# Transposing q and k on VectorE instead of TensorE: sliding-window attention with a gMLP block, one core

## The chip, the cores and the metric

The kernel runs on one core of one Trainium2 chip. The metric is the device time of one execution in microseconds (us). Most executions of one kernel agree within a few tenths of a per cent to one per cent. An execution more than 1.5% above the fastest of its kernel counts as slow; ratios below use the others ("fast runs") alone. The medians that are quoted are over all runs of a kernel, slow ones included; they hold one slow run in e6, e8, e11 and e17, two in e15, and none elsewhere.

PE is TensorE (matmuls), PEld its weight loads, DVE is VectorE, ACT is ScalarE, POOL is GpSimd, SP is SyncE, which only issues transfers. HBM is the memory outside of the core, SBUF the memory inside it, PSUM the accumulators behind PE.

## The reference, cut to what matters

Eight batches, eight heads, 576 tokens, 64 features per head. A token attends to itself and to the 63 tokens before it; a gMLP block with a spatial mixing matrix over the tokens follows.

```python
q, k, v: (8, 8, 576, 64) fp32, normal * 0.1
scores = q @ k.T / 8, kept where 0 <= i - j < 64
x      = softmax(scores) @ v, heads side by side: (8, 576, 512)
h      = relu(x @ w_in)                  # w_in (512, 1024)
u, v   = h[..., :512], h[..., 512:]
v_n    = (v - mean) / sqrt(var + 1e-6)
v_s    = w_spatial @ v_n + b_spatial     # w_spatial (576, 576)
out    = (u * v_s) @ w_out               # w_out (512, 512)
```

A score is a sum of 64 products of order 0.01, some 0.08 in size, divided by 8; so the scores are near zero and the softmax is nearly uniform over the window. **The comparison with the reference cannot see a wrong order of q's and k's tokens.**

## The kernel before

A batch goes through five attention steps (T transposes, S scores, E exponential and mask, P weighted values and denominators, N normalization to x), four of which take two heads each; the fifth takes the last 64 queries of all heads. Then come V and U (the halves of h), LN, G (spatial mixing, times u) and O (output). From the third batch on, the PE stream interleaves the attention of batch i, V, U and G of batch i−1 and O of batch i−2.

q, k and v come in as fp32, 256 bytes at a time, and are cast to fp16 by POOL (by ACT and DVE for the first batch). PE transposes q and k, DVE copies the result out of PSUM, and the scores contract 64 features in one matmul:

```python
def emit_T(b, s):                        # cut: the remainder step s == 4
    tp = psp.tile([128, 1024], f16, tag="tp", bufs=1, ...)
    for c in range(4):
        nc.tensor.transpose(tp[:, 512+128*c:640+128*c], Kh[:, c, 2*s:2*s+2, :], id16[:, :])
    for c in range(4):
        nc.tensor.transpose(tp[:, 128*c:128*c+128],     Qh[:, c, 2*s:2*s+2, :], id16[:, :])
    qk = apool.tile([128, 1024], f16, tag="qk", bufs=6, ...)
    nc.vector.tensor_copy(qk[:, :], tp[:, :])
...
# emit_S: 16 matmuls a step, on 64-row tiles of the array
for h in (0, 1):
    d = slice(64*h, 64*h+64)
    nc.tensor.matmul(sc[r:r+64, h, c0:c1], qk[d, 512+64*kap:576+64*kap], qk[d, c0:c1], ...)
...
# order of a steady iteration
st[2] += [LN] + [U0, U1] + [G0];  st[3] += [U2, G1, U4, G2];  st[4] += [U3, G3, G4]
...
# emit_O
nc.scalar.copy(ob[0:jn, :], po[0:jn, :])                      # ob: 3 buffers
(nc.scalar if b < 2 else nc.sync).dma_start(out[...], ob[0:jn, :])
```

The softmax here doesn't subtract the row's maximum and nothing guards it: scores larger than these inputs give would overflow.

## Time and profile before

The median is 251.62 us (251.4 to 252.29, three runs).

| Reading | Value | View of the profile |
|---|---|---|
| busy PE / DVE / ACT / POOL | 227 / 155 / 152 / 122 of 249.3 us | page, part 1 |
| one steady iteration (first V matmul to the next batch's) | 25.9 us, PE busy 25.6 | windows |
| first V matmul of batch 0 / of batch 1 | 30.1 / 71.3 us | timeline of PE |
| longest PE wait | 4.4 us near 64 us | waits |
| eight transposes of a step on PE | 0.45 us | timeline of PE |
| sixteen score matmuls of a step | 0.35 us | timeline of PE |

From the page of the kernel before: busy times with instruction counts; then the span in 40 slices with a digit for tenths busy, for PE, DVE, the granted clock of PE and the DMA; then two DMA queues with packets, MB and share of the DMA engines' time.

```profile
PE 227.3 (91%) x2588; PEld 116.8 (47%) x2588; DVE 155.3 (62%) x317; ACT 152.2 (61%) x266; POOL 122.1 (49%) x183
...
PE   7784996996399999999999999999999999999893
...
DVE  6453277562459782887479556966597659755630
...
PEclk9999799799569999999999999999999999999998
DMA  8999999999999996992389948995499040014005
...
q1 hardware_dynamic: 114720, 34.88, 70.1%
q0 software_dynamic: 1840, 2.24, 5.2%
```

A slice is 6.2 us. PE is full from the 12th slice (69 us) on, so a steady iteration is worth what its PE work is worth. Ahead of that PE has gaps, the granted clock is lower after the longest of them (digits 5 and 6, 62 to 75 us), and the DMA is busy throughout.

The windows view of the kernel before, one steady iteration (stretch, length, busy time and count of PE, PEld, DVE, ACT, POOL, granted clock, DMA share, GB/s). A DMA share may read over 1.

```profile
150.60:176.50 25.90, 25.57 (x317) 13.23 (x315) 19.11 (x36) 17.78 (x32) 14.96 (x20) 1.00 0.85 183
```

The timeline of PE before (start, duration, instruction, count): the transposes of one step and what follows, and the scores of one step and what follows. The difference of two starts is what a group costs the stream.

```profile
97.89 0.40 PE L210 MATMUL tp_2_1850<-id_130,hk_1219 128*128 128x128 f16 x4
98.12 0.39 PE L213 MATMUL tp_2_1850<-id_130,hq_1218 128*128 128x128 f16 x4
98.34 0.38 PE L330 MATMUL pv_0_1862<-win_179,x_0_1397 128*128 128x512 f16 x1
...
146.62 0.42 PE L242 MATMUL sc_0_2882<-qk_0_2745 64*64 64x128 f16 x16
146.97 0.30 PE L281 MATMUL oz_4_2900<-e2r_2802,onesK 128*64 128x256 f16 x2
```

The transposes cost 98.34 − 97.89 = 0.45 us of PE, the scores 146.97 − 146.62 = 0.35 us. This is what the change wants to trade.

### The profile page before, as it was taken

The numbers are of one execution on the slowest core, as the hardware profiler recorded it, in microseconds if no ns is written. First come the engines' busy times: TensorE is split into PE (matmuls) and PEld (weight loads), VectorE is DVE, ScalarE is ACT, GpSimd is POOL, SyncE is SP. The second block draws the span as 40 slices with busy tenths as digits, with TensorE's granted clock in tenths as the row PEclk, the third lists the DMA queues.
The fourth block names the chain that finished last, engine by engine and source line by source line (L and its number), as shares of the span: only waits on it lengthen the run. The fifth ranks groups of instructions, "written<-read, shape, count | busy, mean of one in ns | idle before, by whom it ended". The sixth has DMA issues, their size and how long they took to land.

```text
span 249.3 us, 6391 instructions
## 1 busy us (share of the span) xinstructions
PE 227.3 (91%) x2588; PEld 116.8 (47%) x2588; DVE 155.3 (62%) x317; ACT 152.2 (61%) x266; POOL 122.1 (49%) x183
## 2 busy tenths in 40 slices
PE   7784996996399999999999999999999999999893
PEld 3442453553254464436544554455445544553351
DVE  6453277562459782887479556966597659755630
ACT  3373484446447666766785577756776677767423
POOL 3469638875499695369016592469135900000000
PEclk9999799799569999999999999999999999999998
DMA  8999999999999996992389948995499040014005
GB/s 159 218 184 208 216 204 229 191 201 276 249 199 210 198 178 175 246 206 52 128 192 211 192 128 221 189 198 135 137 216 156 27 165 5 3 42 149 0 3 189
DMA packets 120014, 40.41 MB, mean 162 GB/s; under 512 B 113776, under 2 KB 114864, under 8 KB 119984
## 3 DMA queue, kind: packets, MB, share of 16 engines
q1 hardware_dynamic: 114720, 34.88, 70.1%
q0 software_dynamic: 1840, 2.24, 5.2%
q10 hardware_dynamic: 3424, 2.88, 4.1%
q8 instruction: 20, 0.33, 0.6%
q14 instruction: 10, 0.08, 0.1%
HBM read 32.79 MB, written 9.44 MB: 169 GB/s over the span
## 4 chain that ended last, share of the span: by engine, by line
PE 60%; DVE 13%; ACT 9%; DMA 8%; SPq 3%; POOL 2%; issue 2%; ACTq 1%; POOLq 0%
SPq L68 3%; DMA nv_80<-in_v_dram 2%; DMA out_dram<-ob_0_1033 2%; DMA out_dram<-ob_1_3433 2%; DMA nq_78<-in_q_dram 2%; ACTq L407 1%; PE ps_0_804 L382 1%; PE warm_583 L114 1%; PE pv_0_1308 L330 1%; PE ps_0_4590 L382 1%; PE ps_0_4237 L382 1%; DVE mv_172 L336 1%; PE ps_0_3720 L382 1%; PE ps_1_895 L382 0%; PE ps_3_4653 L382 0%
## 5 line engine op out<-in xcount | busy, mean ns | idle before, releaser
L88 POOL CAST hq_2281<-nq_2285 128x512 f16<-128x512 f32 (+1 forms) x5 | 3.2, 635 | 12.8 <-DMA nq_2285<-in_q_dram 12.8
L114 PEld LDWEIGHTS <-scratch 128*128 128x128 f16 x51 | 5.0, 112 | 7.3 <-issue 3.8
L88 POOL CAST hq_3389<-nq_3393 128x512 f16<-128x512 f32 (+1 forms) x5 | 3.9, 797 | 8.8 <-DMA nq_3393<-in_q_dram 8.8
L281 PEld LDWEIGHTS <-onesK 128*64 128x64 f16 x80 | 4.6, 107 | 7.5 <-issue 5.2
L88 POOL CAST hq_2835<-nq_2839 128x512 f16<-128x512 f32 (+1 forms) x5 | 3.6, 720 | 8.3 <-DMA nq_2839<-in_q_dram 8.3
L176 ACT CAST hk_109<-nk_79 128x512 f16<-128x512 f32 x4 | 2.5, 618 | 7.5 <-DMA nk_79<-in_k_dram 7.5
L114 PE MATMUL warm_113<-scratch 128*128 128x512 f16 x16 | 5.5, 524 | 1.3 <-DVE scratch L109 1.3
L81 POOL CAST hv_110<-nv_80 128x512 f16<-128x512 f32 x4 | 2.5, 632 | 8.3 <-DMA nv_80<-in_v_dram 7.3
L88 POOL CAST hv_1729<-nv_1733 128x512 f16<-128x512 f32 (+1 forms) x5 | 3.5, 708 | 4.4 <-DMA nv_1733<-in_v_dram 4.4
L88 POOL CAST hq_1727<-nq_1731 128x512 f16<-128x512 f32 (+1 forms) x5 | 2.9, 609 | 4.6 <-DMA nq_1731<-in_q_dram 4.6
L88 POOL CAST hv_2283<-nv_2287 128x512 f16<-128x512 f32 (+1 forms) x5 | 3.2, 637 | 3.8 <-DMA nv_2287<-in_v_dram 3.8
L81 POOL CAST hv_433<-nv_437 128x512 f16<-128x512 f32 x4 | 2.5, 613 | 5.2 <-DMA nv_437<-in_v_dram 5.1
L88 POOL CAST hv_1184<-nv_764 128x512 f16<-128x512 f32 (+1 forms) x5 | 3.1, 611 | 3.9 <-DMA nv_764<-in_v_dram 3.9
L362 PEld LDWEIGHTS <-win_181 128*128 128x128 f16 x32 | 3.1, 98 | 3.8
L362 PEld LDWEIGHTS <-win_182 128*128 128x128 f16 x32 | 3.1, 98 | 3.8
L88 POOL CAST hv_1220<-nv_1224 128x512 f16<-128x512 f32 (+1 forms) x5 | 3.9, 780 | 2.0 <-DMA nv_1224<-in_v_dram 2.0
L88 POOL CAST hq_1182<-nq_762 128x512 f16<-128x512 f32 (+1 forms) x5 | 3.3, 654 | 3.2 <-DMA nq_762<-in_q_dram 2.7
L81 DVE CAST hq_108<-nq_78 128x512 f16<-128x512 f32 x4 | 1.7, 432 | 4.8 <-DMA nq_78<-in_q_dram 4.8
L281 PE MATMUL oz_3_1153<-e_1_3_1108,onesK 128*64 128x512 f16 x2 | 0.6, 611 | 4.4 <-DVE x_2_1133 L308 4.4
L88 POOL CAST hv_3391<-nv_3395 128x512 f16<-128x512 f32 (+1 forms) x5 | 3.0, 611 | 2.8 <-DMA nv_3395<-in_v_dram 2.8
L88 POOL CAST hv_2837<-nv_2841 128x512 f16<-128x512 f32 (+1 forms) x5 | 3.3, 666 | 2.0 <-DMA nv_2841<-in_v_dram 1.8
L264 ACT ACTIVATE e_1_0_831<-sc_0_813 128x1024 f16<-128x1024 f32 x1 | 1.0, 1023 | 5.2 <-PE sc_0_813 L242 5.2
(1871 smaller groups left out, 940.3 us busy)
## 6 DMA issues: line engine op xcount, KB each, us to landing
nk_79<-in_k_dram SPq DMA_DIRECT2D x9, 128.0 KB, 3.9
nq_78<-in_q_dram SPq DMA_DIRECT2D x9, 128.0 KB, 4.1
nk_436<-in_k_dram SPq DMA_DIRECT2D x9, 128.0 KB, 4.8
nq_435<-in_q_dram SPq DMA_DIRECT2D x9, 128.0 KB, 4.8
nv_437<-in_v_dram SPq DMA_DIRECT2D x9, 128.0 KB, 4.1
nk_763<-in_k_dram SPq DMA_DIRECT2D x4, 256.0 KB, 5.5
nq_762<-in_q_dram SPq DMA_DIRECT2D x4, 256.0 KB, 5.7
nv_764<-in_v_dram SPq DMA_DIRECT2D x4, 256.0 KB, 6.0
```

Source lines behind the costliest of these rows:

```text
L68: eng.dma_start(NAT[b][x][:, 0:4, h, :], SRC[x][b, h, 0:512, :].rearrange("(c p) d -> p c d", p=128))
L81: eng.tensor_copy(F16[b][x][:, 0:4, hs, :], NAT[b][x][:, 0:4, hs, :])
L88: eng.tensor_copy(F16[b][x][0:sn, c, :, :], NAT[b][x][0:sn, c, :, :])
L114: nc.tensor.matmul(t[:, :], scratch[:, 0:128], scratch[:, :], start=True, stop=True)
L176: nc.scalar.copy(o, i)
L264: nc.scalar.activation(e2[:, :, :], sc[:, :, :], AF.Exp, bias=0.0, scale=0.125)
L281: nc.tensor.matmul(oz[64 * h:64 * h + 64, 1, 0:n], onesK[:, :], e2[:, h, 0:n], start=True, stop=True)
L330: nc.tensor.matmul(pv[0:jn, :], xcol(b, r, j), w_in_sb[r][:, 512:1024], start=(r == 0), stop=(r == 3))
L336: nc.vector.bn_aggr(mv_t[b % NSB][0:jn, j, :], st6[0:jn, 0:6])
L362: nc.tensor.matmul(pu[:, :], w_in_sb[r][:, 128 * m:128 * m + 128], X[b, r][:, :], start=(r == 0), stop=(r == 3))
L382: nc.tensor.matmul(ps[:, :], VN[b, kk][0:kn, 128 * m:128 * m + 128], wspT[kk][0:kn, 0:512], start=(kk == 0), stop=(kk == 4))
L407: (nc.scalar if b < 2 else nc.sync).dma_start(out[b, 128 * j:128 * j + jn, :], ob[0:jn, :])
```

## The change

Intent: take the transposes off PE and the casts of q and k off POOL, and read HBM in long rows.

- q and k are loaded with 18 consecutive tokens per partition (4.6 KB of fp32 in a row) and cast to fp16 by the DMA itself.
- DVE transposes them in 32x32 blocks. A partition holds tokens 18·i to 18·i+17, so one block gives tokens c, 18+c, 36+c, ... of 32 features. To put the tokens in order, the output is written with a step of 18 elements, 36 bytes.
- DVE leaves the 64 features of a head in two sets of 32 rows, so each score product becomes a pair of 32-row matmuls that accumulate.
- In a steady iteration G comes behind nearly all of U.

```diff
-    def emit_T(b, s): ... nc.tensor.transpose(...) ... nc.vector.tensor_copy(qk, tp)
+    def load_qk(b, x, hp):
+        s = SRC[x][b, 4*hp:4*hp+4, :, :].rearrange("g (i c) d -> (g i) (c d)", c=18)
+        nc.gpsimd.dma_start(NAT[b, x][:, hp, :, :, :].rearrange("p c e d -> p (c e d)"), s)
+
+    def turn(b, x, hp, half):
+        cs = slice(9 * half, 9 * half + 9)
+        o = TR[b, x][:, hp, :, :].rearrange("p e (i c) -> p c e i", c=18)
+        nc.vector.transpose(o[:, cs, :, :], NAT[b, x][:, hp, cs, :, :])
...
+        return [lambda e=e: nc.tensor.matmul(
+            out, TR[b,"k"][rows, hp, e, 64*key:64*key+64], TR[b,"q"][rows, hp, e, q0:q1],
+            start=(e == 0), stop=(e == 1), tile_position=(32*g, r)) for e in (0, 1)]
...
-            st[2] += [LN] + [U0, U1] + [G0];  st[3] += [U2, G1, U4, G2];  st[4] += [U3, G3, G4]
+            st[2] += [LN] + [U0, U1, U2];     st[3] += [G0, U3, G1, U4];  st[4] += [G2, G3, G4]
...
-        ru = mpool.tile([128, 512], f32, tag="ru", bufs=3, ...)
+        ru = mpool.tile([128, 512], f32, tag="ru", bufs=5, ...)
```

(Also cut: a fourth PSUM buffer for U, V, G and O, the two halves of w_in loaded apart, the loads of v and their casts as before but in a new order, and the fill of batch 1's steps, which takes two units of batch 0 ahead of each step instead of one.)

## The prediction

> **What bounds it now.** From 93 to 221 us the kernel is bound by TensorE. In the windows view the four full batch iterations (first output projection to first output projection) last 26.2, 26.1, 25.9 and 25.8 us, with PE busy 25.5 to 25.7 us of each; DVE is busy 18.5, ACT 18. The last batch with attention takes 24.6. At the front, DMA bounds: its share reads over 1.0 up to 93 us, 128 KB loads take 4 to 5 us, and the first V matmul starts at 30.1 us. Between 60 and 64.6 us PE waits 4.4 us for x_2, held behind ACT output copies that wait for 5 us output DMAs; then the granted clock is 0.66 (60 to 75 us).
>
> **PE per iteration (timeline).** Removed: four groups of eight 128-column transposes at 56 ns, 0.45 us each, 1.8 us; the remainder's transposes and the mode change they cause, 0.44. Sum −2.2 us. Added: 32-row pairs double the score matmuls from 16 to 32 per step, still four at once on different tiles. Sixteen now take four groups of 56 ns, so four more groups cost 0.22 us, four times: +0.9. The remainder goes to eight tiles at once, about even. The Trainium skill ("TensorE: Matmul & The Clock Gate", Part 3) says row tiles run concurrently with starts 4 ns apart; today's 64-row score matmuls agree (3 to 4 ns), and the trace has no 32-row ones. Net −1.3.
>
> **G behind U.** G0 takes 1.9 us from its first matmul to the end where its siblings take 1.08: 0.8 lost waiting for the normalized tiles. One more U (0.86) runs in between, but two transposes (instead of one 0.65 us copy) now stand on DVE before normalization: I count −0.4.
>
> **DVE.** Out: copies 3.1 us per iteration. In: eight transposes of 128x576. The trace has none; the skill's "VectorE: DVE Perf Modes" (The three transpose paths) gives 311 ns for 128x128 bf16; with one element per cycle, as a 512-element fp32 copy's 0.69 us suggests, I estimate 0.65 to 0.75 us each, 5.5 in all. DVE rises to about 21 of 24.5 us: not the bound, but g_2 behind two transposes can hold a PSUM slot, +0.3. ACT +0.4 (three exps for the remainder). POOL loses ten casts (about 6 us).
>
> Iteration: 26.0 − 1.3 − 0.4 + 0.3 = 24.6 us. Five iterations (the last 23.5): −7 us. Tail: one U fills the normalization wait, −1.
>
> **Front.** q and k go from 256 B packets to rows of 4.6 KB; the DMA-cast weights moved 2.24 MB (output bytes) in 5.2% of the span, 173 GB/s, so a batch's q and k take some 7 us of DMA instead of 12. First scores about 9.5 us (8.7 now, as four heads must land), then ACT paces some 3 us per step; first V at 24 to 25 instead of 30. Batch 1 waits about 2 us for its eight transposes on DVE. With DMA relieved, the 4.4 us wait and the cold clock after it go. Together −12 us (range −6 to −16).
>
> **Predicted: 232 us**, 8 in 10 within 225 to 241. Faster by over 2%: 0.95; within 2%: 0.04; slower: 0.01.
>
> **What shows it.** Iterations near 24.6 us with PE still over 95%; score steps near 0.48 us of PE; transposes near 0.7 us; first V near 24.5 us; DMA share below 0.8 from 30 us on; no 4 us PE wait near 60 us.
>
> **What would make it wrong.** Transposes with the 36-byte output stride costing over 1.1 us make DVE the bound (25 us per iteration or more); 32-row pairs not overlapping add 0.9 us more per iteration; cast loads slower than 173 GB/s delay the front.

## The result, and the profile after

The changed kernel takes **345.79 us** (344.99 to 347.89, four runs) against 251.84 of the kernel before beside it: ratio 1.3764, 95% interval 1.3703 to 1.3826. It passes the comparison with the reference and is 38% slower. Ratios here and below are the mean time of one kernel's fast runs over that of the other's of the same rounds, so not quite the ratio of the medians that are quoted.

The same lines of the page of the changed kernel, then the chain of work that ended last and two groups of instructions (busy us, mean ns):

```profile
PE 240.2 (70%) x2899; PEld 118.1 (34%) x2899; DVE 279.8 (81%) x329; ACT 152.9 (44%) x283; POOL 87.7 (25%) x138
...
PE   5073885058702767599678967796759695999995
...
DVE  4978359995499699978999799969996999877450
...
PEclk9566999556955699969698989699978969899999
...
q1 hardware_dynamic: 41504, 16.52, 21.0%
q0 software_dynamic: 7024, 11.68, 19.6%
...
DVE 52%; PE 28%; ACT 8%; issue 6%; DMA 3%; POOL 2%; ACTq 0%; POOLq 0%
...
L76 DVE STREAM_TRANSPOSE tq<-nq 128x576 f16<-128x576 f16 x32 | 82.7, 2760 | 0.0
L76 DVE STREAM_TRANSPOSE tk<-nk 128x576 f16<-128x576 f16 x32 | 81.7, 2729 | 0.0
```

DVE went from 155 to 280 us, 52% of the chain is DVE, and the two lines at the end say why: 64 transposes of 2.7 us each, 164 us in all by their durations. The prediction had counted 0.65 to 0.75 us each, some 45 us. The other columns did what was expected: POOL fell from 122 to 88 us and packets from 114,720 to 41,504 on the first queue.

One iteration in the windows view, and the waits of PE (for what, us in total, times, longest):

```profile
189.20:225.80 36.60, 29.16 (x356) 13.86 (x356) 33.98 (x39) 18.18 (x35) 11.05 (x15) 0.86 0.43 98
...
PE sc L202 <- DVE tq L76: 28.2, 3, 12.2
PE oz L265 <- DVE x L293: 22.0, 9, 9.2
PE po L387 <- DVE g L369: 19.2, 9, 3.8
PE ps L366 <- DVE vn L336: 18.9, 9, 3.3
```

An iteration is now 36.6 us with DVE busy 34.0. Only the first wait names a transpose. The others name x, g and vn, small DVE operations that stand in DVE's order behind a pair of transposes (5.1 us): an overloaded engine shows up under the names of whatever queues on it. The granted clock is 0.86 here, with PE pausing; it was 1.00 before and is 1.00 in e2 below, which does the same PE work without these pauses in 24.2 us of busy time. Here PE is busy 29.2 us.

Where the 95.5 us between the two profiled spans (249.3 and 344.8) lie, by the first V matmul of each batch (V0, V1, V7); later rows are explained below. Each row is one profiled execution. Up to the first output, near 55 us, e4 and e18 below are the same program as the kernel before; their V0 is 29.4 and 32.8 us, and V1 of e4 is 69.2. So in this kernel differences of up to some 3 us in V0 or V1 between two profiles are not separated.

| Kernel | V0 | V0 to V1 | V1 to V7 | from V7 to the end | span |
|---|---|---|---|---|---|
| before | 30.1 | 41.2 | 154.8 | 23.2 | 249.3 |
| after | 42.7 | 72.4 | 206.9 | 22.8 | 344.8 |
| e2_contig (no stride, wrong token order) | 27.2 | 47.6 | 147.2 | 22.9 | 244.9 |
| e5_pairs (32-bit words, right order) | 27.1 | 47.7 | 149.0 | 22.9 | 246.7 |
| e17_spout (e5 and a new front) | 27.7 | 31.2 | 149.8 | 22.7 | 231.4 |

### The profile page after: what moved, and what is told of

Same layout as the page of the kernel before. It is cut to its first block, busy times and chain, and to the rows that moved or that the text cites. A ratio compares the mean times of both kernels' runs of the same rounds, so it can differ in the third digit from the quotient of the medians.

```text
span 344.8 us, 6862 instructions
## 1 busy us (share of the span) xinstructions
PE 240.2 (70%) x2899; PEld 118.1 (34%) x2899; DVE 279.8 (81%) x329; ACT 152.9 (44%) x283; POOL 87.7 (25%) x138
## 3 DMA queue, kind: packets, MB, share of 16 engines
q1 hardware_dynamic: 41504, 16.52, 21.0%
q0 software_dynamic: 7024, 11.68, 19.6%
HBM read 32.79 MB, written 9.44 MB: 122 GB/s over the span
## 4 chain that ended last, share of the span: by engine, by line
DVE 52%; PE 28%; ACT 8%; issue 6%; DMA 3%; POOL 2%; ACTq 0%; POOLq 0%
DVE tk L76 18%; DVE tq L76 16%; PE po L387 11%; PE pv L314 5%; DVE x L293 4%; DVE vn L336 4%; PE ps L366 4%; DVE g L369 3%; PE sc L202 3%; DVE st L319 3%; DVE e L251 2%; ACT vs L317 2%; PE oz L265 2%; DMA wnat<-in_moe_w_spatial_dram 2%; PE oz L275 1%
## 5 line engine op out<-in xcount | busy, mean ns | idle before, releaser
L76 DVE STREAM_TRANSPOSE tq<-nq 128x576 f16<-128x576 f16 x32 | 82.7, 2760 | 0.0
L76 DVE STREAM_TRANSPOSE tk<-nk 128x576 f16<-128x576 f16 x32 | 81.7, 2729 | 0.0
L366 PE MATMUL ps<-wspT,vn 128*128 128x512 f16 (+1 forms) x160 | 46.8, 421 | 22.3 <-DVE vn L336 18.9
L387 PE MATMUL po<-wout,g 128*128 128x512 f16 (+1 forms) x160 | 48.4, 446 | 19.2 <-DVE g L369 19.2
L115 POOL COPY vs<-vn 64x1024 f16<-64x1024 f16 (+1 forms) x44 | 40.5, 921 | 60.5 <-PE oz L275 33.4
L242 ACT ACTIVATE e<-sc 128x1024 f16<-128x1024 f32 x32 | 32.7, 1022 | 41.6 <-PE sc L202 40.5
L202 PE MATMUL sc<-tq,tk 32*64 32x128 f16 (+2 forms) x1152 | 29.0, 249 | 28.9 <-DVE tq L76 28.2
L314 PE MATMUL pv<-win,x 128*128 128x512 f16 (+1 forms) x160 | 39.3, 392 | 0.0
L319 DVE BATCH_NORM_STATS2 st<-vs 128x6 f32<-128x512 f16 (+1 forms) x40 | 27.5, 687 | 13.2 <-ACT vs L317 12.8
L346 PE MATMUL pu<-x,win 128*128 128x512 f16 x128 | 33.9, 404 | 0.0
L283 ACT ACTIVATE ln<-oz 128x512 f32<-128x512 f32 (+1 forms) x40 | 22.3, 557 | 25.8 <-PE oz L275 24.6
```

Of the source, the lines that this page charges most:

```text
L76: nc.vector.transpose(o[:, cs, :, :], NAT[b, x][:, hp, cs, :, :])
L115: nc.gpsimd.tensor_copy(o, i)
L202: return [lambda e=e: nc.tensor.matmul(out, TR[b, "k"][rows, hp, e, 64 * key:64 * key + 64], TR[b, "q"][rows, hp, e, q0:q1], start=(e == 0 ...
L242: nc.scalar.activation(e2[:, :, :], sc[0][:, :, :], AF.Exp, bias=0.0, scale=0.125)
L314: nc.tensor.matmul(pv[0:jn, :], xcol(b, r, j), w_in_sb[r][:, 512:1024], start=(r == 0), stop=(r == 3))
L319: nc.vector.bn_stats(st6[0:jn, 0:6], vs[0:jn, :])
```

## The experiments

Theory A for the slowdown: the 36-byte step of the writes makes each transpose slow. Rivals: B, the block transpose is slow by itself in this shape; C, it is slowed by the other engines and the DMA beside it.

### e1_turns: the transposes by themselves

No attention at all: six times each, alone on the core, the transposes of this kernel and variants of them, and plain copies (output wrong, 133.34 us).

```diff
+ for r in (1, 2, 3, 6, 9, 18):                 # tokens per run: step of 2*r bytes
+     nc.vector.transpose(t[:, 0, :].rearrange("p (k i r) -> p k r i", i=32, r=r),
+                         src[:, :, 0, :].rearrange("p (k r) d -> p k r d", r=r))
```

> The VectorE transpose alone, six of each form in a row, nothing else on the chip but the write-out of zeros (the output is wrong on purpose). In the changed kernel a 128x576 fp16 transpose took 2.61 to 2.86 us with a start-to-start pitch of 2.3 to 2.5 us. Theory A (write stride: the output columns of a block lie 18 tokens, 36 bytes, apart, so each write goes to another SBUF line; the Trainium skill, SBUF - State Buffer, names 16-byte lines): the as-is form repeats 2.5 to 2.8 us, contiguous output takes 0.65 to 0.8 us, runs of 2 and 3 tokens (4 and 6 byte steps) also under 0.9 us, 6 tokens (12 bytes) in between, 9 and 18 tokens 2.5 us or more; a plain copy with the 36-byte step is slow as well. Rival B (the transpose itself costs about 4 cycles per element or a fixed 140 ns per 32x32 block, whatever the stride): all fp16 forms of 576 elements take 2.5 us or more, and 128 flat columns take about 0.55 us. Rival C (contention with loads and with GpSimd in the real kernel): even the as-is form takes 0.65 to 0.8 us here.

From the groups of instructions of this run (busy us, mean ns; the first two lines are the kernel's own form with a step of 36 bytes and contiguous, then copies with that step and contiguous, fp32 elements with a step of 72 bytes and contiguous, a step of 36 bytes on the read side only, and 128x128 flat):

```profile
L70 DVE STREAM_TRANSPOSE asis<-src 128x576 f16<-128x576 f16 x6 | 15.8, 2639 | 0.2
L73 DVE STREAM_TRANSPOSE asis<-src 128x576 f16<-128x576 f16 x6 | 4.7, 779 | 0.2
...
L96 DVE COPY copy<-src 128x576 f16<-128x576 f16 x6 | 8.4, 1399 | 0.2
L93 DVE COPY copy<-src 128x576 f16<-128x576 f16 x6 | 1.9, 310 | 0.2
...
L105 DVE STREAM_TRANSPOSE wide<-src 128x576 f32<-128x576 f32 x6 | 7.6, 1258 | 0.2
L101 DVE STREAM_TRANSPOSE wide<-src 128x576 f32<-128x576 f32 x6 | 4.7, 778 | 0.2
...
L89 DVE STREAM_TRANSPOSE readstep<-src 128x576 f16<-128x576 f16 x6 | 7.2, 1199 | 0.2
L82 DVE STREAM_TRANSPOSE flat<-src 128x128 f16<-128x128 f16 x6 | 1.9, 312 | 0.2
```

The steps in between, six transposes each, one by one from the trace: 2 bytes 779 ns, 4 bytes 814, 6 bytes 1132, 12 bytes 2092, 18 bytes 2692, 36 bytes 2640.

Theory A holds and B and C fall. The same transpose takes 779 ns when it writes contiguously and 2639 ns with the kernel's step, alone on the core; the kernel's 2.7 us adds only some 4% for all that runs beside it. The block transpose is not slow by itself: written contiguously it is short, and a plain copy slows with the same step too, from 310 to 1399 ns. But the step adds 1.09 us to the copy and 1.86 us to the transpose, so it is not one cost for both; why stays open. The cost rises with the step and is level from 18 bytes on. One size was forecast wrongly: a step of 6 bytes was to stay under 0.9 us and took 1.13. The width counts too: 4-byte elements at 72 bytes cost 1258 ns, half of what 2-byte elements at 36 bytes cost for the same count, and twice the data.

The Trainium skill ("SBUF — State Buffer", Specifications) says that SBUF has 16-byte lines that need two or more hits each for full bandwidth and that each crossing to a new line pays. The level from 18 bytes on agrees with a line of that size; the rise that starts at 6 bytes, with two or more elements still in a line, does not. The page gives no size of the penalty; here it is 1.9 us per instruction of 576 elements. The skill's "VectorE: DVE Perf Modes" (The three transpose paths) gives 311 ns for 128x128 bf16; the trace has 312 for fp16. The passage cut from the prediction rested the estimate on a copy of 512 fp32 elements in 0.69 us, and no trace shown then has such a copy: the DVE casts of 512 fp32 elements took 0.43 us. The figure that the prediction used was right, but it is that of a contiguous output.

### e2_contig: the changed kernel without the stride

One line of the change differs: tokens are written in the order in which they come. q and k are then permuted in the same way, so the scores pair wrong tokens; the result is wrong and still within tolerance. The times of all engines are those of the real work.

```diff
-        o = TR[b, x][:, hp, :, :].rearrange("p e (i c) -> p c e i", c=18)
+        o = TR[b, x][:, hp, :, :].rearrange("p e (c i) -> p c e i", c=18)
```

> The changed kernel with one line altered: the transposes write contiguous columns (tokens end up in the wrong order, the result is wrong on purpose); every instruction count, size and dependency stays. Theory A: each transpose takes 0.65 to 0.8 us, DVE falls to about 21 us per batch, and the time falls to the predicted 232 us (225 to 241), showing that the rest of the prediction held. Rival B: the transposes stay near 2.75 us and the time near 345 us. Rival D (the transposes are not the only cause: the pairs of 32-row matmuls or the cast loads are slow as well): transposes become short but the time stays above 245 us.

Measured: 247.53 us (246.57 to 248.49, two runs), ratio 0.9857 (0.9782 to 0.9931). From its page (one group), its windows view and its timeline of PE:

```profile
L76 DVE STREAM_TRANSPOSE tk<-nk 128x576 f16<-128x576 f16 x32 | 22.6, 744 | 0.0
...
150.00:174.20 24.20, 24.20 (x355) 12.13 (x354) 19.75 (x38) 17.73 (x35) 10.23 (x15) 1.00 0.69 149
...
151.87 0.64 PE L202 MATMUL sc<-tq,tk 32*64 32x128 f16 x32
152.44 0.41 PE L265 MATMUL oz<-e,onesK 128*64 128x512 f16 x2
```

That one line is worth 98 us, more than the whole loss. The transposes are short as Theory A of the forecast said, but the time is not the forecast 225 to 241 us; it lies over the 245 of Rival D. Without the stride the steady part is what the prediction said: 24.2 us per iteration (24.6 predicted), and 32 score matmuls in 152.44 − 151.87 = 0.57 us against 0.35 for 16, which is the +0.22 us per step of the prediction. (The skill's "TensorE: Matmul & The Clock Gate", Part 3, says that 32-row tiles run concurrently; these 0.57 us agree.) But the kernel gains 1.4% and not 8%: V1 comes at 74.8 us, later than before (71.3). The front, worth −12 us in the prediction, did not come. That is the second question, taken up from e5 on.

### e3_run3: three tokens per partition and row

Loads of runs of three tokens (768 bytes of fp32), so that the step is 6 bytes. This needs four loads where one did. The token order is right by its access patterns.

```diff
-        s = SRC[x][b, 4*hp:4*hp+4, :, :].rearrange("g (i c) d -> (g i) (c d)", c=18)
+        for g in range(4):
+            s = SRC[x][b, 4*hp+g, :, :].rearrange("(k i c) d -> i k (c d)", i=32, c=3)
```

> A correct version: a partition takes runs of 3 tokens (768-byte pieces, six per partition) instead of 18, so a transposed block is written with a 6-byte step. The loads become four per half of the heads, with six times as many pieces for GpSimd to describe. Theory A: transposes under 0.9 us, time between 228 and 245 us, faster than before. Rival B: still about 345 us. If the smaller pieces cost what the 256-byte ones of before did, the front end lies some 5 us behind that of the contiguous variant.

Measured: 267.12 us, ratio 1.0629 (1.0577 to 1.0682), where 228 to 245 us and transposes under 0.9 us were forecast. The transposes take 1.11 to 1.13 us as in e1, and an iteration 25.5 us. The loss is new: POOL issues 128 loads for q and k at 0.57 us each, 72 us in all; V0 comes at 38.4 and V1 at 87.4 us. The group of the k loads (busy us, mean ns):

```profile
L73 POOL DMA_DIRECT2D nk<-in_k_dram x64 | 36.2, 573 | 10.3 <-DMA nk<-in_k_dram 6.0
```

### e4_gorder: the new order of G and U alone

The kernel before with only the order of U and G of the change. Its `ru` tiles keep three buffers, because five don't fit into SBUF there.

```diff
-            st[2] += [LN] + [U0, U1] + [G0];  st[3] += [U2, G1, U4, G2];  st[4] += [U3, G3, G4]
+            st[2] += [LN] + [U0, U1, U2];     st[3] += [G0, U3, G1, U4];  st[4] += [G2, G3, G4]
```

> The kernel before with only the order of G and U changed in batches 1 to 7 (three ru buffers as before, since five do not fit beside its fp32 tiles). My prediction counted 0.4 us per batch, up to 0.8 (the wait of G0 for the normalized tiles), for six full batches and about 1 us in the tail: time 247.5 to 249.5 us, that is 1 to 2% faster than before. If the wait only moves to another place, the time stays within 0.5%.

Measured: 249.24 us, ratio 0.9949 (0.9884 to 1.0015). Its iteration in the windows view is 25.5 us against 25.9, the 0.4 us of the prediction. But that holds for the iterations in the middle only: the first after V1 takes 28.0 us against 27.1, the last 24.5 against 23.8, and V1 to V7 is 154.7 us against 154.8. The new order moved the time and saved none of it there.

### e5_pairs: the change mended, with the tokens in order

DVE moves two fp16 features as one 32-bit word. One transpose then has half as many elements, 4 bytes wide, with a step of 72 bytes. A row holds the even and odd feature of a pair side by side, so a 32-row score matmul takes the even ones, the other the odd ones, each reading with a step of 4 bytes. As the comparison with the reference can't see token order, the layout was worked through with an index model; it puts the tokens of the change and of e5 in order. No run shows it.

```diff
-        o = TR[b, x][:, hp, :, :].rearrange("p e (i c) -> p c e i", c=18)
-        nc.vector.transpose(o[:, cs, :, :], NAT[b, x][:, hp, cs, :, :])
+        o = TR[b, x][:, hp, :, :].rearrange("p t e -> p (t e)").bitcast(f32)
+        n = NAT[b, x][:, hp, :, :].rearrange("p c d -> p (c d)").bitcast(f32)
+        nc.vector.transpose(o.rearrange("p (i c) -> p c i", c=18)[:, cs, :],
+                            n.rearrange("p (c d) -> p c d", d=32)[:, cs, :])
```

> The changed kernel with correct token order and its 4.6 KB load rows, but the transposes move 32-bit words, each a pair of neighbouring fp16 head dimensions: half the columns, 288 per transpose, written with a 72-byte step; the score matmuls then read even and odd dimensions with a 4-byte step. From the isolated forms (576 columns of fp32 with a 72-byte step 1.26 us, flat forms' fixed part about 0.18) I estimate 0.72 us per transpose, as many as before. Theory A (2-byte writes to scattered lines are the cost) expects transposes near 0.75 us and the time of the contiguous variant, 245 to 250 us. If TensorE reads the 4-byte step at half rate, each score step (0.64 us with the next one's wait in the contiguous variant) grows by 0.3 us or more, 1.3 us per batch, and the time is 255 us or more. Rival B (any transpose is slow in the real kernel) fell already with the isolated run.

Measured: 248.82 us, ratio 0.9926 (0.9841 to 1.001). One group and one iteration:

```profile
L77 DVE STREAM_TRANSPOSE tq<-nq 128x288 f32<-128x288 f32 x32 | 19.9, 699 | 0.1
...
151.00:175.60 24.60, 23.99 (x355) 12.46 (x354) 19.11 (x38) 17.71 (x35) 10.20 (x15) 1.00 0.66 146
```

A transpose of the same data takes 0.70 us instead of 2.7, and by the index model the order is right. The iteration is 24.6 us. Its front is that of e2 (V0 27.1, V1 74.8).

### e6_ob6, e7_wsp, e8_pairs_front: two repairs of the front

In e2, PE stands 3.2 us for w_spatial near 35 us, and 4.8 us for x near 66 us, where ACT waits for a buffer of an output copy. e6 is e2 with six output buffers instead of three; e7 is e2 with w_spatial (and the first half of w_in) loaded earlier; e8 is e5 with both.

```diff
-        ob = mpool.tile([128, 512], f32, tag="ob", bufs=3, ...)      # e6, e8: bufs=6
-        if s == 2: load_win(1)
-        if s == 3: load_win(0)
-        if s == 4: load_wsp()
+        if s == 1: load_win(1); load_wsp()                           # e7, e8
+        if s == 2: load_win(0)
```

> The contiguous variant (token order wrong on purpose) with one number changed: six output buffers instead of three. In the contiguous variant ACT stood 3.2 us and then PE 4.8 us from 60.9 us on, since the fourth output copy had to wait for an output DMA among the bursts of prefetch loads, and the cold clock followed. Theory F1 (output buffers cost the front): the 4.8 us wait goes, time 240 to 243.5 us. Rival F2 (the wait is only the symptom of loads that saturate the DMA, another wait takes its place): time within 1.5 us of 247.5.

> The contiguous variant (token order wrong on purpose) with the weight loads issued earlier: the V half of w_in and the spatial weights after step 1, the U half after step 2. In the contiguous variant PE waits from 31.8 to about 36 us for the spatial weights, whose loads GpSimd issues only from 26.0 us on, and batch 1's loads queue behind them. Theory F3: the W transposes follow V at once, normalization and batch 1 start 4 us earlier, time 242 to 244.5 us. Rival: the earlier loads delay the batch-0 casts or loads and V starts later than 27.2 us; time unchanged.

> A correct kernel that joins the 32-bit pairs, the six output buffers and the earlier weight loads. If the two front effects add up (4 us each) and TensorE reads the pairs at full rate: 236 to 242 us, some 5% faster than before. If pairs are slow for TensorE, 250 us or more; if only one front effect holds, 242 to 246 us.

| Run | time, us | ratio, 95% | V0 | V1 |
|---|---|---|---|---|
| e6_ob6 (token order wrong) | 244.28 | 0.9709 (0.9623 to 0.9795) | slow profile | slow profile |
| e7_wsp (token order wrong) | 245.81 | 0.979 (0.9723 to 0.9857) | 30.0 | 74.8 |
| e8_pairs_front | 246.69 | 0.978 (0.968 to 0.9881) | 30.6 | 70.6 |

The profiled run of e6 was slow, so its details are not used. e7 does away with the wait for w_spatial, but V0 comes 2.8 us later and V1 at the same time as in e2: the wait had moved, not gone. In e8 the longest wait of PE for x is 1.5 us where e5 has 4.9, so the 4.8 us wait of e2 goes with these two repairs. Each repair is worth one per cent or so; both e6 and e7 lie between the two times that had been forecast for them, and e8 outside of its 236 to 242 us. Most of the missing 12 us stays missing.

### e9_dveshift, e10_front3, e11_vf1: rearranging, and holding back one load

Two theories for the front. W: new waits in the issue order of the changed kernel eat the gain. D: the DMA is full, and transfers that run ahead take it from those that are needed. e9 is e8 and moves the shifted copies of batch 0's values from POOL to DVE; e10 is e9 and puts four transposes of batch 1 ahead of LN of batch 0 and spreads the filler work as the kernel before does; e11 is e10 and has one fp32 buffer for v instead of two, so that the v of batch 2 cannot be loaded before batch 1's is cast.

```diff
-            shift_pair(0, s, pool_copy)
+            shift_pair(0, s, dve_copy)                  # e9, e10, e11
+    for f in turns(1)[0:4]: f()                         # ahead of emit_LN(0): e10, e11
-        att_step(1, s, todo, 2, 1 if s else 0)
+        att_step(1, s, todo, 1, 1 if s else 0)          # e10, e11
-        VF[b] = inpool.tile([...], f32, tag="vf", bufs=2, ...)
+        VF[b] = inpool.tile([...], f32, tag="vf", bufs=1, ...)   # e11
```

> The two-feature transposes of e5 with six output buffers and early weights (e8), and the 64-token shifted copies of the values of batch 0 moved from GpSimd to VectorE. In e8 GpSimd made the copies for step 2 only at 22.2 us, behind eleven weight loads that it issued and waited for, and the TensorE waited 1.8 us and then ran six cold warm-up matmuls. Theory W (the front lost its gain to new waits in the issue order of the changed kernel): V0 moves from 30.6 to about 28, first V of batch 1 from 70.6 to 68 to 70, total 1 to 2.5 us under e8. Rival D (the front is bound by DMA bytes; the waits only show where it is felt): V0 moves but the first V of batch 1 stays at 70 to 71 and the total is within 0.8 us of e8.

> e9, and the first four transposes of batch 1 placed on VectorE before the normalization of batch 0, the other four behind step 0, and filler work of batch 0 spread over the steps of batch 1 as in the kernel before (one unit ahead of each step instead of two; the changed kernel used all up by step 2). Theory W: the 1.9 us wait for tq near 43 us goes, and of the 5 us of waits for x between 61 and 71 us at least 2 go; first V of batch 1 at 65 to 68, total 2 to 5 us under e9, some 240 to 243 us. Rival D: the waits move onto the casts of V and the DMA, first V of batch 1 stays within 1.5 us of e9's.

> e10 with one fp32 buffer for the values instead of two: the load of the values of batch 2 then waits for the casts of batch 1 (about 50 us) instead of running ahead of everything at 30 us. Theory D (transfers that run ahead steal the DMA from those that are needed now): the values of batch 1 land earlier, first V of batch 1 1 to 3 us earlier than in e10. Theory W: within 1 us of e10. If the single buffer starves the steady state, iterations lengthen over 24.7 us and the casts of V wait for the DMA.

| Run | time, us | ratio, 95% | V0 | V0 to V1 |
|---|---|---|---|---|
| e9_dveshift | 251.61 | 0.9991 (0.9902 to 1.008) | 35.4 | 44.2 |
| e10_front3 | 250.61 | 0.9944 (0.9875 to 1.0014) | 32.8 | 44.8 |
| e11_vf1 | 242.0 | 0.9621 (0.9583 to 0.9659) | 35.2 | 33.9 |

e9 missed both expectations: it got slower. The copies on POOL had held back the weight loads that POOL issues behind them. With the copies gone, POOL issues the weights from 4.8 us on (14.7 in e8), and the values of batch 0 land late: ACT waits 2.7 and 4.5 us for them near 20 and 27 us. A step that looked like a pure loss was a gate for the DMA. e11, with the values of batch 2 held back, takes 34 us from V0 to V1 instead of 45, far more than the 1 to 3 us that D had forecast. That speaks for D. (e10 met neither forecast: V1 at 77.6 us, 2.0 ahead of e9.)

### e12_order, e13_pairs_vf1, e14_before_nv1: does holding back explain it?

e12 is e11 with the weights nearly in their old places (w_spatial one step earlier, the second half of w_in last) and the copies back on POOL. e13 is e5 with one v buffer and nothing else. e14 is the kernel before with one fp32 v buffer.

```diff
# e12, against e11
-            shift_pair(0, s, dve_copy);  s == 1: win(1), wsp;  s == 2: win(0)
+            shift_pair(0, s, pool_copy); s == 2: win(1);  s == 3: wsp;  s == 4: win(0)
# e13, against e5; e14 does the same to the kernel before
-  tag="vf", bufs=2
+  tag="vf", bufs=1
```

> e11, with the weights loaded where the changed kernel loads the first half of w_in (after step 2's copies on GpSimd), w_spatial one step earlier than there and the second half of w_in last, and the shifted copies of batch 0 back on GpSimd, which holds the weight loads behind the values of batch 0. In e9 to e11 the weights were issued from 4.8 us on and the values of batch 0 landed late: V0 at 35 us. Theory D (what is loaded ahead of its need takes the DMA from what is needed): V0 back at 26 to 29, first V of batch 1 at 61 to 66, total 232 to 239 us. Theory W: V0 at 27 to 28 but new waits for w_spatial or for tq behind it; first V of batch 1 at 68 to 72, total 240 to 244 us.

> e5 with one fp32 buffer for the values instead of two and nothing else changed. Theory D: the values of batch 2 no longer run ahead at 30 us, so the values of batch 1 and w_spatial land earlier; first V of batch 1 at 67 to 72 instead of 74.8, total 241 to 246 us. Theory W: nothing, 247.5 to 250 us.

> The kernel before, with one fp32 buffer for the values instead of two. If loads that run ahead cost its front what they cost the changed kernel's, it too gets faster by 2 to 6 us, and that part of the later versions' gain is not the change's. If the gain is only there with the cast loads, it stays within 1.5 us of before, or gets slower in the steady state, where GpSimd casts every value tile late.

| Run | time, us | ratio, 95% | V0 | V0 to V1 |
|---|---|---|---|---|
| e12_order | 247.51 | 0.9873 (0.9836 to 0.991) | 27.2 | 46.4 |
| e13_pairs_vf1 | 249.18 | 0.9926 (0.9883 to 0.9969) | 27.4 | 47.8 |
| e14_before_nv1 | 251.4 | 1.0003 (0.996 to 1.0047) | 31.3 | 39.8 |

Theory D as it stood falls: holding the values back does nothing by itself (e13), and V1 of e12 is 73.6 us where D had forecast 61 to 66. The timelines of e12 show why. The line of PE tells of a wait for the shifted copies of the values of batch 1, the lines of POOL that the last cast waited for its load to land and that five copies of 5.3 us in all stood behind it:

```profile
50.63 0.27 PE L277 MATMUL oz<-e,vs 128*64 128x64 f16 x2 [6.77 <-POOL vs L117]
...
44.26 0.61 POOL L117 CAST vn<-vf 128x512 f16<-128x512 f32 x1 [5.41 <-DMA vf<-in_v_dram]
47.54 0.61 POOL L117 CAST vn<-vf 64x512 f16<-64x512 f32 x1 [2.66 <-DMA vf<-in_v_dram]
48.10 5.33 POOL L117 COPY vs<-vn 64x1024 f16<-64x1024 f16 x5
```

With one buffer the values of batch 1 wait for the casts of batch 0, the weights wait for POOL, and from 10 to 20 us the DMA share is 0.46 (it is 0.97 in e2). What is not moved then is missing at 44 us.

### e15_order2 and e16_v2early: the DMA busy, in the order of need

e15 has two v buffers again, issues the values of batch 1 right behind those of batch 0, the weights and the first q and k of batch 1 in the order of need, and makes the shifted copies of two chunks right behind their casts. The values of batch 2 are issued from ACT's queue after U of batch 0. e16 undoes the last point only.

```diff
# e15, against e12
+    new_v(1); load_v_chunk(1, c, nc.sync) for c in range(5)     # ahead of the steps of batch 0
+        s == 1: win(1);  s == 2: q, k of batch 1, first four heads;  s == 3: wsp;  s == 4: win(0)
-        load_v_chunk(2, c, nc.sync)
+        load_v_chunk(2, c, nc.scalar)                           # e16: nc.sync
```

> e12 left the DMA half idle from 12 to 24 us (the values of batch 1 waited for the one buffer, the weights for GpSimd), and the values of batch 1 landed at 44 and 47 us, with 5.3 us of shifted copies still to make behind them. Here nothing idles and nothing runs ahead: two value buffers again, values of batch 1 issued right behind those of batch 0, weights and q and k of batch 1 in the order of need, values of batch 2 issued from the ScalarE's queue after U of batch 0 (about 40 us), and the shifted copies of a chunk pair right behind its casts. Theory O (the front is the order in which one busy DMA serves it: neither idling nor running ahead): V0 at 27 to 29, first V of batch 1 at 61 to 66, total 232 to 238 us. Theory W (the chain of engine waits sets it whatever the DMA does): first V of batch 1 at 69 to 73, total 240 to 245 us.

> e15 with one thing put back: the values of batch 2 issued from the queue of all value loads, so that they start as soon as the values of batch 0 are cast (about 22 us). Theory O: they take the DMA from w_spatial, w_in and q and k of batch 1 just then (1.18 MB are some 5.5 us of it at the 213 GB/s of the traces); first V of batch 1 3 to 6 us later than in e15 and the total 3 to 6 us longer. Theory W: within 1 us of e15.

e15: 245.21 us, ratio 0.9664 (0.9574 to 0.9754), two of its four runs slow (243.29 and 242.05 fast, 247.14 and 248.3 slow). e16: 245.96 us, ratio 0.9791 (0.971 to 0.9871). V0 27.4 and 27.6, V1 70.5 and 73.9. For e15 these are the numbers of Theory W (V1 at 69 to 73, 240 to 245 us), not of O. Between fast runs e16 takes 3.4 us more, as O had forecast for it, but the two ratios' intervals overlap and the slowest run of e15 lies above all of e16's; whether running ahead costs anything by itself stays open. e15's profile showed something else. From 27 to 40 us its PE is nearly without a gap (V0 to the first G in 11 us), then it loses what it won. The longest waits of PE in the first 100 us, the waits of ACT between 30 and 72 us, and the issues in its timeline:

```profile
PE oz L267 <- DVE x L295: 10.0, 7, 5.7
PE sc L204 <- ACT e L244: 3.3, 1, 3.3
...
ACT ru L350 <- DMA vf<-in_v_dram: 4.8, 1, 4.8
ACT zi L293 <- DMA vf<-in_v_dram: 4.6, 2, 3.0
...
37.12 5.32 ACTq L90 DMA_DIRECT2D vf<-in_v_dram  x5
```

ACT issues five loads and stands 5.3 us over it. Most of that does not come from a DMA that was full before: SP takes 4.3 us to issue five such loads in e17 (its timeline below) after 5.2 us with a DMA share of 0.55, while one store takes 0.34. Then ACT stands 1.6 and 3.0 us ahead of the normalization of x. Each of these two lies between ACT's copy of an output tile of batch 0 and the issue of its store, from ACT's own queue. In e16, where ACT issues no loads, it stands 6.5 us ahead of such a normalization and 4.6 us ahead of an output copy, again at the issue of a store. PE waits 3.3 us for the exponentials behind the loads and 5.7 us for the x behind the second store. The kernel before also issues the outputs of its first two batches from ACT, but there ACT stands at most 0.9 us at a time around those of batch 0.

### e17_spout and e18_before_spout: no transfer issued from ACT

e17 is e15 with all outputs issued from SP, and the values of batch 2 from SP behind the first output of batch 0. e18 is the kernel before with its outputs issued from SP.

```diff
-        (nc.scalar if b < 2 else nc.sync).dma_start(out[...], ob[0:jn, :])
+        nc.sync.dma_start(out[...], ob[0:jn, :])
```

> In e15 the front was 4 us ahead of all others until 40 us and then lost it on the ScalarE: five issues of the values of batch 2 held it 5.3 us (37.1 to 42.5), and two output stores of batch 0 issued from it stood 1.6 and 3.0 us behind transfers still under way, which the scores' exponentials and the x tiles waited out (TensorE waits of 3.3 and 5.7 us). Here all outputs are issued from the SyncE's queue, as from batch 2 on anyhow, and the values of batch 2 from there too, behind the first output of batch 0 (about 55 us). Theory Q (an engine that issues a transfer in order stands still while the DMA is full; that, not the DMA itself, ate the front): the waits of 3.3 and 5.7 us go, first V of batch 1 at 62 to 66, total 233 to 238 us. Rival (the work of the steps itself sets it): first V of batch 1 at 69 to 71, total within 1 us of e15's fast runs (242.7 us).

> The kernel before with the outputs of its first two batches issued from the SyncE's queue instead of the ScalarE's. Theory Q in the kernel before: its wait of 4.4 us for x near 64 us shrinks by 1 to 3 us, total 1 to 3 us less. If the outputs queue up behind the value loads there (SyncE issues in order too), it is the same within 1 us or slower.

e17: **235.25 us** (233.06 to 237.62, six runs), ratio 0.9357 (0.9311 to 0.9402). e18: 256.13 us, ratio 1.0226 (1.0191 to 1.0261). The first fence is of e17: two of its waits of PE in the first 100 us, the stretch from 50 to 60 us in the windows view, one steady iteration, and the issue of five loads in the timeline of SP. The second is of e18: its longest wait of PE in the first 100 us, then a line each of the timelines of ACT and SP.

```profile
PE oz L267 <- DVE x L295: 5.3, 6, 2.0
PE sc L204 <- DVE tq L77: 4.3, 1, 4.3
...
50.00:60.00 10.00, 6.37 (x154) 4.04 (x154) 7.98 (x15) 7.23 (x14) 5.76 (x7) 0.91 1.00 252
...
135.90:160.60 24.70, 24.09 (x356) 12.53 (x356) 19.55 (x38) 18.12 (x35) 10.55 (x15) 1.00 0.66 146
...
137.26 4.27 SPq L90 DMA_DIRECT2D vf<-in_v_dram  x5
```

```profile
PE oz L281 <- DVE x L308: 8.5, 1, 8.5
...
67.29 0.58 ACT L406 COPY ob<-po 128x512 f32<-128x512 f32 x1 [7.19 <-DMA out_dram<-ob]
...
63.35 6.05 SPq L407 DMA_DIRECT2D out_dram<-ob  x5
```

The waits of 3.3 and 5.7 us are gone and none took their place; V1 comes at 58.9 us instead of 70.5. This is the best version, 6.4% faster than the kernel before, with q and k in the right order by the index model. Against e15 three things changed at once: the queue of the stores, the queue of the loads of batch 2's values, and their start (49.5 us instead of 37.1). With the last the DMA share falls, to 0.93 and 0.70 in the stretches from 30 to 40 and 40 to 50 us (1.10 and 1.06 in e15). So that ACT's place, and not the emptier DMA, made the gain is argued from the two waits and not shown; no run has the one without the other.

In the kernel before the same edit does harm (the interval is clear of 1). There SP issues the loads of q, k and v of the next batches in its order, and the outputs of batch 0 come behind them: ACT has copied the first at 57.0 us, SP issues it at 63.4. With three output buffers, ACT's fourth copy then waits 7.2 us for one to come free (0.9 in the kernel before), and PE 8.5 us for x (4.4 before). V1 comes at 76.8 us instead of 71.3, but 2.7 us of this are there at V0 already, ahead of any output; that part the edit does not explain. e17 has fewer loads on SP, because q and k come through POOL, places the values of batch 2 behind an output on purpose, and has six output buffers; whether more buffers would mend e18 was not tried. So the move is not a rule: it depends on what the stores then stand behind.

## Why the prediction was wrong, point by point

- **The step that failed is "In: eight transposes of 128x576 ... I estimate 0.65 to 0.75 us each, 5.5 in all".** They took 2.75 us each, 22 us per batch. The estimate took a figure for a contiguous output (312 ns for 128x128 in the trace) and scaled it by size, although the diff shows an output step of 36 bytes. e1 shows the step as the cause alone on the core, e2 in the kernel: without it 744 ns, and 98 us less.
- "Not the bound" followed from it. DVE was estimated at 21 of 24.5 us and was busy 34 of 36.6.
- The prediction named this risk ("Transposes with the 36-byte output stride costing over 1.1 us make DVE the bound") and gave it next to no weight: 0.01 for slower. A named cost that no trace had measured, eight times a batch on an engine that was already 70% busy, deserved more.
- **PE per iteration, −2.2 and +0.9: right.** e2 has 0.57 us per score step against 0.35, and PE is busy 24.2 us of an iteration of 24.2 (25.6 of 25.9 before; 24.6 was predicted). The whole V1 to V7 is 7.6 us shorter in e2, 5.8 in e5; predicted was −7 for five iterations.
- **G behind U, −0.4: not borne out.** Alone in e4 (with three `ru` buffers, not five) it shortens the iterations in the middle (25.5 against 25.9 us), but V1 to V7 is 154.7 us against 154.8.
- "32-row pairs not overlapping" and "cast loads slower than 173 GB/s" did not happen as far as seen: first scores at 10.4 us in e2 against the predicted 9.5; the queue of the cast loads moved 11.68 MB in 27.3% of the span of e2, 175 GB/s by the sum that gave the prediction its 173.
- **"First V at 24 to 25 instead of 30": half right.** Without the stride it is 27.1 to 27.7 us where the weights keep their places or nearly so (30.0 and 30.6 in e7 and e8).
- **"With DMA relieved, the 4.4 us wait and the cold clock after it go": wrong as reasoned.** The change cuts packets, not bytes: 32.79 MB are read from HBM in both kernels, and the DMA share of e2 from 40 to 60 us is 1.18 and 1.16 against 1.22 and 1.19 before. What was freed was filled at once. The share falls only in the steady state (0.69 against 0.85), where the DMA is no bound. The wait came back as 4.8 us in e2. There ACT stands 3.2 us for an output buffer ahead of it; with six buffers and earlier weights (e8) no wait for x is over 1.5 us. e15 has such a wait again, 5.7 us, and e17 none over 2.0: V0 to V1 31.2 us against 41.2.
- With the stride mended and the front put in order, the sum of the prediction is nearly there: front −12.4 us (V1 at 58.9 against 71.3), later parts −5.0 and −0.5, together −18 (231.4 against 249.3) where −20 was predicted. It took repairs that were not in the change, so that the front meets the predicted −12 is luck. How much of the front these repairs would bring to the old layout is open; the two that were tried on the kernel before brought nothing (e14) or harm (e18).

What stays open: why narrow writes with a step cost as much as they do (only sizes and steps were varied); whether loads that run ahead cost something by themselves (e15 against e16 is within the spread of e15's runs); which of ACT's two kinds of transfer in e15, the five loads or the stores behind them, cost more, since e17 removed both; how much of e17 is the emptier DMA; and the 2.7 us at V0 of e18.

## What to carry to other kernels

Before costing an engine's instruction from another instance of it, compare the access patterns, the output's above all; if no trace has the pattern, measure it alone first, for six instructions of each form settle it. If 2-byte data must be scattered, look for a pairing that moves it as 4-byte words and let the reader take the step (2.7 to 0.7 us here). And when a change relieves a full DMA at the start of a kernel, ask which loads will fill the gap, and look at which engine issues the transfers: what stands behind the issue on an engine that the critical path needs (e15), and what the transfers stand behind elsewhere (e18).

## What the Trainium skill lacked or had wrong

- "VectorE: DVE Perf Modes", The three transpose paths: 311 ns for 128x128 is right for a contiguous output (312 here), but nothing says what an output step costs: 779 ns become 814, 1132, 2092, 2692 and 2640 at steps of 4, 6, 12, 18 and 36 bytes for 128x576 fp16.
- "SBUF — State Buffer", Specifications, has the 16-byte lines but no size of the penalty, and a note on the same page lets 2-byte data stride eight elements for free: here a step of three elements (6 bytes) already costs 45% and six elements (12 bytes) 2.7 times. The width matters as well, which the page doesn't say: 4-byte elements at 72 bytes cost 1.6 times their contiguous form (1258 against 778 ns), 2-byte elements at 36 bytes 3.4 times.
- "DMA: Bandwidth & Descriptors", Issuing engines are not separate DMA queues, says that the issuing engine changes only the time it takes to initiate a transfer, "which is usually small relative to the DMA itself". One by one this agrees: a store took 0.34 us to issue and a load of v 1.06 (five in 5.3 us on ACT in e15), where the median load of v from ACT took 5.3 us to land. What the section does not say is what a row of them does to an engine that computes: the 5.3 us stood ahead of ACT's exponentials, and PE waited 3.3 us for these.
